# Feed-forward behind a blocked attention: from feature rows to token rows, on one core

## The chip, the core and the metric

The kernel runs on 1 core of one Trainium2 chip. The metric is the device time of one execution in microseconds (us): lower is better. The core has TensorE (PE, matrix products), VectorE (DVE), ScalarE (ACT), GpSimd (POOL), SyncE (SP, which here issues the transfers) and 16 DMA engines. Matrix products land in PSUM, which has 8 banks of 128 partitions by 2 KB; everything else works from SBUF, 128 partitions.

## The reference

A linear attention with decay, in blocks, whose output is the input of a highway feed-forward.

```
q, k, v: [4, 8, 768, 64] f32          lam: [8]
for each block of 64 positions:
    intra = (qb @ kb.T * Dmask) @ vb          Dmask[i, j] = lam ** (i - j) for i >= j, else 0
    inter = (qb * lam ** (pos + 1)) @ kv_state
    out[block] = intra + inter
    kv_state = lam ** 64 * kv_state + (kb * lam ** (63 - pos)).T @ vb
x = out, as [3072 tokens, 512 features]
H = maximum(x @ w_h, 0)
T = 1 / (1 + exp(-(x @ w_t + b_t)))
result = T * H + (1 - T) * x                  f32, [3072, 512]
```

The result can be written as (H - x) * T + x, which is how both kernels do it.

## The kernel before

The 3072 tokens are cut into 12 tiles of 256 (4 batches of 3). Every instruction is issued in an order written out by hand: the string PLAN is a list of tokens, each a step with its tile, its part, after "@" its engine, and after "=" its PSUM banks (0 to 6; a further bank holds the state kv). Each engine runs its own instructions in this order, and so does SP's DMA queue with its loads and stores; an instruction that waits holds up all that stand behind it on its engine.

The steps of a tile: `Lk`, `Lq`, `Lv` load the inputs in two halves of 4 heads, 256 KB each (`load`, line 173; each contiguous run is 2 tokens of one head, 512 bytes). `CK` casts k to bf16; `CQ` and `CV` scale q and v by powers of lambda (`scale`, line 190), on POOL mostly. `TK` and `TQ` turn k and q on PE, eight transposes each (`trans`, line 204); `EK` and `EQ` copy them out of the bank (lines 101 for ACT, 103 for the others). `SS` makes the scores of one half of the heads together with updates of the state (lines 216, 221); `M` masks the scores on DVE (line 255); `KE` copies the state out; `I` and `A` make the inter and intra parts of the output (lines 271, 281); `D` copies it to xT, with features in partitions and tokens in the free dimension, and permutes the tokens while it writes.

Feed-forward: `W` loads the two weights (line 177), four loads of 512 KB in 2 KB rows; `WC` casts them. `F` is `block` (line 300): a 128x128 piece of a weight is the stationary operand and 256 tokens of xT stream past it, 8 matmuls for a bank of two feature groups; 4 blocks a tile, two for each weight. `H` is `relu` (line 305): max(h, 0) - xT, from the bank and SBUF. `G` is the sigmoid (line 314), two instructions a block, with the bias as one number for each partition, back into the bank. `X` is the gate (line 318), which reads that bank. `R` turns xT and the gated th back into token rows on PE, adding them in the bank (line 347; 327 for the last tile, which goes in two halves of 128 tokens). `E` copies the result out, `ST` stores it (lines 356 and 337), from SP.

`Z` are idle matmuls of 512 columns (line 366), which keep PE busy while it waits at the start. The SBUF tiles rotate through the numbers of buffers in BUFS; five each for the loaded q, k and v.

Of the kernel before, what the change touches and what calls it, by code (L numbers as in the profile page):

```python
# [17 lines left out]
Lk.0.0 Lv.0.1 Lv.0.0 Lq.0.0 Lk.0.1 Lq.0.1 Lv.1.1 CK.0.0@POOL Lq.1.0 Z.12=0 TK.0.0=0 Lq.1.1 CV.0.0@DVE Lk.1.0  # L18
CQ.0.0@POOL EK.0.0@DVE Lv.1.0 CV.0.1@DVE CK.0.1@ACT Lk.1.1 Z.11=1 TQ.0.0=1 B=2 EQ.0.0@ACT CQ.0.1@POOL W.0.1 W.0.0
Z.6=0 TQ.0.1=3 TK.0.1=4 EQ.0.1@DVE U.0.0 EK.0.1@ACT W.1.1 S.0.0=56 KE.0.0@DVE S.0.1=01 CQ.1.2@POOL W.1.0 M.0.0.1 Z.1=3  # L20
U.0.1 I.0=34 M.0.1.1 KE.0.1@ACT Lk.2.1 M.0.0.0 A.0.1 M.0.1.0 TQ.1.2=0 Lq.2.1 CV.1.2@DVE CK.1.2@ACT EQ.1.2@ACT Lq.2.0
Z.8=1 TK.1.2=1 A.0.0 EK.1.2@DVE Lk.2.0 D.0.0@DVE Z.3=5 SS.1.1=56 WC.0.0.1@ACT WC.0.0.0@POOL M.1.1.0 KE.1.0@ACT
WC.0.1.0@POOL D.0.1@ACT Lv.2.1 WC.0.1.1@DVE Z.4=0 SS.1.0=01 M.1.1.1 I.1=35 KE.1.1@ACT Lv.2.0 F.0.0.0=4 WC.1.1.0@DVE PT
M.1.0.1 Lk.3.1 F.0.1.0=6 M.1.0.0 WC.1.0.0@POOL WC.1.0.1@ACT Lk.3.0 WC.1.1.1@DVE A.1.1 A.1.0 BC F.0.0.1=1 H.0.1 Lq.3.1
D.1.1@ACT H.0.0 D.1.0@ACT F.0.1.1=0 Lq.3.0 CQ.2.2@POOL F.1.0.0=2 Lv.3.0 G.0.1@ACT CK.2.2@DVE F.1.0.1=6 Lv.3.1
G.0.0@ACT X.0.1@DVE TQ.2.2=5 Lq.4.0 X.0.0@DVE TK.2.2=4 EQ.2.2@ACT CV.2.2@POOL F.1.1.0=3 Lq.4.1 EK.2.2@DVE G.1.0@ACT
H.1.0 SS.2.0=01 Lk.4.1 H.1.1 CK.3.2@POOL SS.2.1=54 Lk.4.0 M.2.0.1 F.1.1.1=2 KE.2.0@ACT M.2.1.0 Lv.4.0 TK.3.2=3 M.2.1.1
CQ.3.2@POOL G.1.1@ACT I.2=15 M.2.0.0 Lv.4.1 A.2.1 X.1.0@DVE A.2.0 Lk.5.0 R.0=40 D.2.0@ACT D.2.1@DVE CV.3.2@POOL
TQ.3.2=6 E.0.0@ACT Lk.5.1 F.2.1.1=1 E.0.1@ACT EQ.3.2@DVE Lq.5.1 EK.3.2@ACT X.1.1@DVE F.2.1.0=5 CQ.4.2@POOL Lq.5.0
R.1=40 H.2.1 SS.3.1=62 Lv.5.0 F.2.0.0=3 CK.4.2@POOL KE.3.0@ACT M.3.1.1 Lv.5.1 E.1.1@ACT M.3.1.0 SS.3.0=52 E.1.0@ACT  # L30
H.2.0 Lq.6.0 TQ.4.2=0 KE.3.1@ACT CV.4.2@POOL M.3.0.1 TK.4.2=6 G.2.1@ACT Lq.6.1 F.2.0.1=4 M.3.0.0 EQ.4.2@ACT EK.4.2@DVE
Lv.6.0 I.3=32 A.3.0 CK.5.2@POOL A.3.1 Lk.6.1 SS.4.1=56 D.3.0@ACT D.3.1@DVE TK.5.2=0 KE.4.0@ACT M.4.1.1 Lk.6.0
F.3.0.0=2 G.2.0@ACT CQ.5.2@POOL EK.5.2@DVE Lv.6.1 SS.4.0=36 H.3.0 F.3.0.1=0 Lq.8.0 M.4.0.0 CV.5.2@POOL M.4.0.1
TQ.5.2=2 Lk.9.0 G.3.0@ACT F.3.1.0=3 X.2.1@DVE Lq.7.0 EQ.5.2@ACT X.2.0@DVE F.3.1.1=6 CQ.6.2@POOL M.4.1.0 Lq.7.1
KE.4.1@ACT I.4=14 H.3.1 G.3.1@ACT R.2=25 Lk.8.1 X.3.0@DVE A.4.0 E.2.1@ACT X.3.1@DVE A.4.1 Lk.7.1 SS.5.0=30 E.2.0@ACT
D.4.0@DVE CK.6.2@POOL SS.5.1=56 D.4.1@ACT Lk.7.0 TQ.6.2=2 M.5.0.0 KE.5.0@ACT CV.6.2@POOL TK.6.2=1 M.5.1.1 Lv.7.0
EQ.6.2@ACT F.4.1.0=4 M.5.0.1 Lv.7.1 EK.6.2@ACT F.4.0.0=3 H.4.1 Lk.8.0 M.5.1.0 I.5=62 SS.6.1=01 H.4.0 Lq.8.1 A.5.0
KE.6.0@ACT M.6.1.0 CQ.7.2@POOL R.3=45 Lv.9.1 A.5.1 M.6.1.1 SS.6.0=30 D.5.0@ACT Lv.8.0 F.4.0.1=1 M.6.0.0 D.5.1@ACT
M.6.0.1 Lk.9.1 TQ.7.2=6 G.4.0@ACT CK.7.2@POOL F.5.0.0=3 Lq.10.1 EQ.7.2@ACT F.4.1.1=2 H.5.0 Lk.10.1 E.3.1@ACT X.4.0@DVE
TK.7.2=0 CV.7.2@POOL G.4.1@ACT I.6=63 ST.0 KE.6.1@DVE F.5.0.1=5 X.4.1@DVE Lv.8.1 F.5.1.0=1 G.5.0@ACT CK.8.2@POOL  # L40
EK.7.2@DVE Lq.9.0 A.6.0 E.3.0@ACT H.5.1 A.6.1 SS.7.1=20 Lq.9.1 D.6.0@ACT D.6.1@DVE TK.8.2=4 M.7.1.1 F.6.1.0=1 Lv.9.0
EK.8.2@ACT X.5.0@DVE CK.9.2@POOL F.6.1.1=6 KE.7.0@DVE Lk.10.0 CQ.8.2@POOL H.6.1 R.4=30 SS.7.0=54 Lk.11.1 E.4.0@ACT
F.5.1.1=1 E.4.1@ACT M.7.0.1 G.6.1@ACT ST.4 M.7.1.0 TK.9.2=3 Lq.10.0 M.7.0.0 TQ.8.2=0 G.5.1@ACT CV.8.2@POOL F.6.0.0=4
EQ.8.2@DVE Lk.11.0 KE.7.1@ACT X.5.1@DVE I.7=25 EK.9.2@ACT Lq.11.0 A.7.0 H.6.0 A.7.1 CQ.9.2@POOL SS.8.0=01 X.6.1@DVE
D.7.1@ACT Lv.10.1 SS.8.1=34 M.8.0.1 D.7.0@ACT F.6.0.1=6 KE.8.0@DVE Lq.11.1 CK.10.2@POOL F.7.0.0=5 M.8.1.0 G.6.0@ACT
M.8.1.1 ST.3 TQ.9.2=1 CV.9.2@POOL H.7.0 F.7.1.0=2 EQ.9.2@ACT Lv.10.0 X.6.0@DVE TK.10.2=3 M.8.0.0 ST.1 I.8=45
EK.10.2@ACT CQ.10.2@POOL H.7.1 SS.9.1=61 A.8.1 KE.9.0@ACT M.9.1.0 A.8.0 R.5=02 M.9.1.1 SS.9.0=36 CK.11.2@POOL
E.5.1@DVE F.7.0.1=1 KE.9.1@ACT M.9.0.1 E.5.0@ACT F.7.1.1=2 D.8.0@DVE D.8.1@ACT ST.5 CQ.11.2@POOL M.9.0.0 G.7.0@ACT
Lv.11.1 TK.11.2=6 Lv.11.0 I.9=04 F.8.1.0=5 EK.11.2@ACT ST.2 X.7.0@DVE TQ.10.2=3 G.7.1@ACT H.8.1 CV.10.2@POOL F.8.0.0=1
EQ.10.2@ACT R.6=65 H.8.0 A.9.1 X.7.1@DVE A.9.0 SS.10.1=31 D.9.0@ACT D.9.1@DVE F.8.1.1=2 E.6.1@ACT M.10.1.1 F.9.1.0=0  # L50
E.6.0@DVE G.8.1@ACT M.10.1.0 ST.6 TQ.11.2=4 CV.11.2@POOL KE.10.0@DVE F.9.1.1=5 EQ.11.2@ACT X.8.1@DVE SS.10.0=16
G.9.1@ACT H.9.1 R.7=32 M.10.0.1 KE.10.1@ACT F.8.0.1=4 X.9.1@DVE E.7.0@ACT M.10.0.0 E.7.1@ACT I.10=06 SS.11.0=53
G.8.0@ACT ST.7 A.10.0 M.11.0.0 A.10.1 SS.11.1=21 D.10.1@ACT X.8.0@DVE F.9.0.0=5 KE.11.0@ACT M.11.1.0 D.10.0@ACT
F.9.0.1=6 M.11.0.1 M.11.1.1 F.10.1.0=4 G.9.0@ACT H.9.0 I.11=20 X.9.0@DVE A.11.0 A.11.1 R.8=31 D.11.0@ACT R.9=56
E.8.0@ACT F.10.0.0=2 E.9.0@DVE E.9.1@ACT E.8.1@ACT D.11.1@DVE ST.9 F.10.1.1=3 H.10.0 ST.8 F.10.0.1=6 H.10.1 G.10.1@ACT
F.12.1.1=5 G.10.0@ACT X.10.1@DVE F.11.1.1=1 F.11.1.0=0 G.12.1@ACT X.10.0@DVE F.11.0.1=2 G.11.1@ACT H.11.1 F.12.1.0=4
R.10=36 G.11.0@ACT H.12.1 X.11.1@DVE F.11.0.0=0 E.10.0@ACT X.12.1@DVE F.12.0.1=4 E.10.1@ACT H.11.0 F.12.0.0=1
G.12.0@ACT X.11.0@DVE ST.10 R.11.1.1=5 H.12.0 R.11.0.2=3 E.11.1.1@DVE X.12.0@DVE E.11.0.2@ACT ST.11.1.1 R.11.1.0=0
ST.11.0.2 E.11.1.0@DVE ST.11.1.0
"""  # L60

BUFS = dict(kf=5, qf=5, vf=5, kb=3, qb=2, vs=3, kT=2, qT=2, m=8, xT4=2, th4=2, xT2=3, xT1=2, th2=2, th1=2, hm2=3, hm1=2, tb2=2, tb1=2, ss=4, o=5, oh=2, oq=1)
# [3 lines left out]
def kernel(  # L66
# [18 lines left out]
    J = 2  # L85
    N = B * NST
# [19 lines left out]
    lam_bc = singles.tile([128, H], F32)  # L106
    A.dma_start(out=lam_bc, in_=lam.partition_broadcast(128))
    bt_r = singles.tile([KC, 128], F32)
    A.dma_start(out=bt_r, in_=moe_b_t.rearrange("(j p) -> j p", p=128))
    id128 = singles.tile([128, 128], BF16)  # L110
    make_identity(nc, id128)
    blank = singles.tile([128, 512], BF16)
    V.memset(blank, 0.0)
    tk_i = singles.tile([128, NST, J], I32)
    P.iota(tk_i, pattern=[[2 * C, NST], [1, J]], base=0, channel_multiplier=J)
    tri = singles.tile([128, J, J, C // J], F32)
    P.memset(tri, 1.0)
    for b in range(2):
        P.affine_select(out=tri[half(b)], in_=tri[half(b)], compare_op=ALU.is_ge, fill=0.0, base=0,
                        pattern=[[-1, J], [1, J], [J, C // J]], channel_multiplier=-J)  # L120
    tri = tri.rearrange("p j i q -> p j (i q)")
    tk_f = singles.tile([128, NST, J], F32)
    V.tensor_copy(tk_f, tk_i)
    id_f = singles.tile([KC, KC], F32)
    V.tensor_copy(id_f, id128[0:KC, 0:KC])
    A.preload_act_table_set("natural_log_exp_and_others")
    ln_bc = singles.tile([128, H], F32)
    A.activation(ln_bc, lam_bc, AF.Ln)
    p_ln = singles.tile([128, NST, H, J], F32)
    V.tensor_tensor(p_ln, in0=ln_bc[:, None, :, None].to_broadcast([128, NST, H, J]),  # L130
                    in1=tk_f[:, :, None, :].to_broadcast([128, NST, H, J]), op=ALU.mult)
    pow_q = singles.tile([128, NST, H, J], F32)
    A.activation(pow_q, p_ln, AF.Exp)
    pow_v = singles.tile([128, NST, H, J], F32)
    A.activation(pow_v, p_ln, AF.Exp, scale=-1.0)
    bt_col = singles.tile([128, KC], F32)
# [4 lines left out]
    kv = ps.tile([128, NP, 128], F32, tag="kv", name="kv", bufs=1)  # L141
    V.memset(kv, 0.0)


    made = {}

    def groups(n, b):
        return ((n,), b) if n < N - 1 else ((n, b), 0)
# [12 lines left out]
    def get(*key):  # L161
        return made[key]
# [7 lines left out]
    def load(x, n, p, eng):  # L170
        b, c = divmod(n, NST)
        hs = heads(p)
        (A if eng else nc.sync).dma_start(out=new((x + "f", n), [128, H, J * D], F32)[:, hs],  # L173
                          in_=SRC[x][b, hs, c * 2 * C:(c + 1) * 2 * C, :].rearrange("h (p j) d -> p h (j d)", j=J))

# [7 lines left out]
    def cast_k(n, p, eng):  # L183
        hs = heads(p)
        copy(eng, new(("kb", n), [128, J, H, D])[:, :, hs].rearrange("p j h d -> p h j d"),
             get("kf", n)[:, hs].rearrange("p h (j d) -> p h j d", j=J))

    def scale(n, p, eng, src, dst, pw):
        z = H if p == 2 else 4
        ENG[eng].tensor_tensor(dst, in0=get(src, n)[:, heads(p)].rearrange("p h (j d) -> p h j d", j=J),  # L190
                               in1=pw[:, n % NST, heads(p), :, None].to_broadcast([128, z, J, D]), op=ALU.mult)

    def cast_q(n, p, eng):
        scale(n, p, eng, "qf", new(("qb", n), [128, J, H, D])[:, :, heads(p)].rearrange("p j h d -> p h j d"), pow_q)

    def cast_v(n, p, eng):
        scale(n, p, eng, "vf", new(("vs", n), [128, H, J, D])[:, heads(p)], pow_v)

# [220 lines left out]
```

## Time and profile before

| | us |
|---|---|
| median of 3 runs | 109.54 |
| lowest and highest run | 109.3 and 109.64 |
| span of the profiled execution | 109.3 |
| line 300 (feed-forward matmuls) in the chain of waits | 28% of the span |
| loads of q in the chain of waits | 11% |
| idle matmuls, busy time and count | 11.8, 43 |
| masks on DVE, busy time and count | 31.1, 48 |
| scalings of q and v on POOL, busy time | 42.6 |

How to read it: a busy time is the time in which an engine had an instruction running; instructions of an engine may overlap a little, so a group's count times its mean can exceed its busy time. The chain of waits is followed back from the last instruction: its shares add to the span. The table in slices of time gives, for 40 equal slices of 2.73 us, each engine's busy tenths (9 is 90% or more), and the DMA engines' mean busy share. HBM reads are 20.98 MB, writes 6.29 MB.

### The profile page before, as it was taken

Reading aid. Unit: us, or ns where it says so; the run is one execution under the profiler, and the core shown is the slowest. Engines: PE = TensorE matmul, PEld = TensorE weight load, DVE = VectorE, ACT = ScalarE, POOL = GpSimd, SP = SyncE. Lnnn points to the kernel's source line nnn. Section 1 sums busy time; section 2 is a strip of 40 time slices with the busy share of each in tenths; the row PEclk is TensorE's granted clock in tenths of the full one; section 3 lists DMA queues with packets and bytes.
Section 4 is the critical chain, followed back from the end, with each engine's and each line's share of the span. In section 5 each row is a group of like instructions: output and inputs, shape, how many; then the busy total and the mean of one; then the engine's idle time right before and its main releaser. Section 6 shows DMA issues by size and latency. Waiting matters only on the chain.

```text
span 109.3 us, 4968 instructions
## 1 busy us (share of the span) xinstructions
PE 99.4 (91%) x2188; PEld 80.6 (74%) x2190; DVE 82.7 (76%) x140; ACT 71.9 (66%) x129; POOL 55.7 (51%) x46
## 2 busy tenths in 40 slices
PE   4986989899999999999999999998999599999950
PEld 1343654688887878889899889896888478899940
DVE  1241595878998696999977989999858958958960
ACT  3304263787866489499579749975696758776940
POOL 6029420427979858959468296499691600000000
PEclk9999999999999999999999999999999999999999
DMA  0899999999999999989999999599999413207264
GB/s 5 233 304 290 291 366 386 312 290 287 290 266 304 287 250 262 302 228 289 296 300 293 305 341 270 181 346 326 321 333 323 170 69 125 73 6 296 94 233 151
DMA packets 42701, 27.59 MB, mean 252 GB/s; under 512 B 1588, under 2 KB 38712, under 8 KB 42680
## 3 DMA queue, kind: packets, MB, share of 16 engines
q1 hardware_dynamic: 42528, 27.27, 85.1%
q8 instruction: 17, 0.28, 1.2%
q14 instruction: 4, 0.03, 0.1%
q10 hardware_dynamic: 152, 0.01, 0.1%
HBM read 20.98 MB, written 6.29 MB: 249 GB/s over the span
## 4 chain that ended last, share of the span: by engine, by line
PE 61%; DMA 11%; DVE 6%; POOL 5%; ACT 5%; issue 4%; SPq 4%; POOLq 0%; DVEq 0%
PE bt L300 15%; PE bh L300 13%; DMA qf<-in_q_dram 11%; PE bs L216 7%; PE bo L281 5%; PE bx L347 5%; PE bspin L366 4%; PE bqtr L204 4%; DVE m L255 3%; SPq L173 3%; PE bktr L204 3%; POOL qb L190 3%; PE bo L271 3%; ACT qT L101 2%; POOL vs L190 2%
## 5 line engine op out<-in xcount | busy, mean ns | idle before, releaser
L300 PEld LDWEIGHTS <-w_b 128*128 128x128 bf16 x416 | 36.3, 98 | 6.4 <-issue 1.8
L255 DVE TENSOR_TENSOR m<-bs,tri 128x512 bf16<-128x512 f32 x48 | 31.1, 682 | 3.8 <-PE bs L216 3.4
L190 POOL TENSOR_TENSOR qb<-qf,pow_q 128x1024 bf16<-128x1024 f32 (+1 forms) x13 | 23.6, 1813 | 11.2 <-DMA qf<-in_q_dram 10.6
L314 ACT ACTIVATE bt<-bt,bt_col 128x256 f32<-128x256 f32 (+1 forms) x52 | 22.0, 432 | 6.9 <-PE bt L300 4.2
L300 PE MATMUL bt<-xT,w_b 128*128 128x256 bf16 (+1 forms) x208 | 24.5, 265 | 1.3 <-ACT qT L101 1.3
L300 PE MATMUL bh<-xT,w_b 128*128 128x256 bf16 (+1 forms) x208 | 25.0, 265 | 0.2 <-issue 0.2
L190 POOL TENSOR_TENSOR vs<-vf,pow_v 128x1024 bf16<-128x1024 f32 x10 | 19.0, 1904 | 5.0 <-DMA vf<-in_v_dram 4.6
L305 DVE SCALAR_TENSOR_TENSOR hm<-bh,xT 128x512 bf16<-128x512 f32 (+1 forms) x26 | 16.5, 643 | 4.0 <-PE bh L300 2.5
L318 DVE TENSOR_TENSOR th<-bt,hm 128x512 bf16<-128x512 f32 (+1 forms) x26 | 16.5, 643 | 2.1 <-ACT bt L314 2.0
L216 PE MATMUL bs<-qT,kT 64*64 64x128 bf16 x384 | 14.2, 218 | 0.6 <-issue 0.3
L101 ACT ACTIVATE xT<-bo 128x512 bf16<-128x512 f32 x16 | 11.5, 749 | 4.6 <-PE bo L281 4.6
L103 POOL CAST kb<-kf 128x1024 bf16<-128x1024 f32 (+1 forms) x10 | 10.0, 995 | 8.1 <-DMA kf<-in_k_dram 6.8
L101 ACT ACTIVATE ss<-kv 128x512 bf16<-128x512 f32 x15 | 8.9, 595 | 7.3 <-PE bs L216 6.1
L366 PE MATMUL bspin<-blank,id 128*128 128x512 bf16 x43 | 11.8, 416 | 1.6 <-POOL id masks.py:199 1.4
L216 PEld LDWEIGHTS <-kT 64*64 64x64 bf16 x384 | 11.0, 106 | 2.9 <-issue 1.4
L101 ACT ACTIVATE o<-bx 128x512 f32<-128x512 f32 x19 | 10.4, 596 | 1.4 <-PE bx L347 1.3
L101 ACT ACTIVATE qT<-bqtr 128x1024 bf16<-128x1024 bf16 (+1 forms) x10 | 9.8, 980 | 1.8 <-PE bqtr L204 1.8
L281 PE MATMUL bo<-m,vs 64*64 64x128 bf16 x384 | 9.4, 219 | 0.7 <-DVE m L255 0.4
L221 PE MATMUL kv<-vs,kb 64*64 64x64 bf16 x320 | 9.2, 196 | 0.2 <-POOL vs L190 0.2
L366 PEld LDWEIGHTS <-id 128*128 128x128 bf16 x45 | 4.3, 105 | 6.4 <-issue 1.7
L204 PE MATMUL bqtr<-id,qb 128*128 128x128 bf16 x96 | 7.5, 220 | 0.9 <-POOL qb L190 0.9
L281 PEld LDWEIGHTS <-vs 64*64 64x64 bf16 x384 | 6.6, 106 | 2.4 <-issue 1.5
(50 smaller groups left out, 109.1 us busy)
## 6 DMA issues: line engine op xcount, KB each, us to landing
kf<-in_k_dram SPq DMA_DIRECT2D x24, 256.0 KB, 5.5
vf<-in_v_dram SPq DMA_DIRECT2D x24, 256.0 KB, 5.4
qf<-in_q_dram SPq DMA_DIRECT2D x24, 256.0 KB, 5.5
out_dram<-o SPq DMA_DIRECT2D x11, 512.0 KB, 4.7
w_f<-in_moe_w_h_dram SPq DMA_DIRECT2D x2, 512.0 KB, 6.6
w_f<-in_moe_w_t_dram SPq DMA_DIRECT2D x2, 512.0 KB, 8.5
out_dram<-oh SPq DMA_DIRECT2D x2, 128.0 KB, 2.0
out_dram<-oq SPq DMA_DIRECT2D x1, 256.0 KB
```

The costliest lines, as they stand in the source:

```text
L101: A.activation(dst, src, AF.Copy)
L103: ENG[eng].tensor_copy(dst, src)
L190: ENG[eng].tensor_tensor(dst, in0=get(src, n)[:, heads(p)].rearrange("p h (j d) -> p h j d", j=J), in1=pw[:, n % NST, heads(p), :, None].t ...
L204: T.transpose(t[:, i, j, :], get(x + "b", n)[:, j, h:h + 2, :], id128)
L216: T.matmul(get("s", n, e, hp // 2)[half(b), hp % 2, j, :], lhsT=get("kT", n)[half(e), hp, j, half(b)], rhs=get("qT", n)[half(e), hp, :, ha ...
L255: V.tensor_tensor(new(("m", n, e, u), [128, 2, J, C]), in0=get("s", n, e, u), in1=tri[:, None].to_broadcast([128, 2, J, C]), op=ALU.mult)
L281: T.matmul(get("o", n, b)[half(e), hp, :], lhsT=get("vs", n)[half(b), 2 * hp + e, j, :], rhs=get("m", n, e, u)[half(b), hp % 2, j, :], sta ...
L300: T.matmul(t[:, r, :], lhsT=w_b[w][:, kc, (2 * u + r) * 128:(2 * u + r + 1) * 128], rhs=get("xT", *g)[:, kc, :], start=(kc == 0), stop=(kc ...
L305: V.scalar_tensor_tensor(new(("hm", g, u), [128, 2, z * C], tag=f"hm{z}"), in0=get("h", g, u), scalar=0.0, in1=get("xT", *g)[:, 2 * u:2 * ...
L314: A.activation(dst[:, r, :], src[:, r, :], AF.Sigmoid, bias=bt_col[:, 2 * u + r:2 * u + r + 1])
L318: ENG[eng].tensor_tensor(new(("th", g), [128, NP, z * C], tag=f"th{z}")[:, 2 * u:2 * u + 2, :], in0=get("tt", g, u), in1=get("hm", g, u), ...
L366: T.matmul(t, lhsT=id128, rhs=blank, start=True, stop=True)
```

## The change

The feed-forward is computed in token rows. For 128 tokens at a time, xT is the stationary operand and 512 columns of a weight stream past it (`block`: 4 matmuls for a bank of 128 tokens by 512 features; parts of 256 columns for the end of the last tile). The result needs no turning back. Instead x itself is turned once (`TX`, `rows`: eight transposes a tile, and `XC`, `evac_x`, a copy to SBUF in bf16).

The bias now runs along the free dimension, so it is written into the bank before the matmuls add to it (`BP`, `begin`): a copy of a 128x512 tile b_bc on ACT (20 times) or DVE (5 times). b_bc is made at the start from three bf16 parts of the bias in a weight tile, by one matmul with ones (`B`, `BB`, `BC`).

`H` writes max(h, 0) - x to y in f32; `G` is one sigmoid instruction of 512 columns without a bias operand, to g in SBUF in f32; `X` multiplies y by g and `Y` adds x, both with all operands in SBUF, on DVE (8 and 12 times) or POOL (17 and 13 times). `ST` stores a tile, five times in two transfers of 119 and 9 rows.

q is loaded in runs of 8 tokens of one head (2 KB), with 32 groups of tokens and 4 heads over the partitions; powers of lambda are laid out to match (pow_q8), the turned q is put in order when it is copied out (`EQ`, strided read, written in order), and `D` copies without a permutation. Lambda is loaded as 8 numbers and spread over the partitions by two small matmuls. Four more idle matmuls stand at the start; the Z tokens have 23 in place of 45.

The order is new: all loads of tiles 0 to 3 stand ahead of the weights, and the feed-forward begins after the inter part of tile 3. Scalings are spread differently (8 of 12 whole scalings of q on POOL before 11, 6 of v before 10).

```diff
-BUFS = dict(..., m=8, xT4=2, th4=2, xT2=3, xT1=2, th2=2, th1=2, hm2=3, hm1=2, tb2=2, tb1=2, ss=4, o=5, oh=2, oq=1)
+BUFS = dict(..., m=8, ss=4, xT=3, xs=3, y=4, g=3, ob=5)
...
+        if x == "q":
+            nc.sync.dma_start(out=new(("qf", n), [128, 2, Q * D], F32)[:, p],
+                              in_=q[b].rearrange("(h e) (c p j) d -> c e p h (j d)", e=2, p=C // NP, j=Q)[c, p])
+            return
...
     def evac_q(n, p, eng):
-        hs = heads(p)
-        copy(eng, new(("qT", n), [128, NP, J, C])[:, hs.start // 2:hs.stop // 2], get("qtr", n, p))
+        hs = slice(0, NP) if p == 2 else slice(2 * p, 2 * p + 2)
+        copy(eng, new(("qT", n), [128, NP, 2 * C])[:, hs].rearrange("e h (p j) -> e h p j", j=Q),
+             get("qtr", n, 2).rearrange("e j (p h) -> e h p j", h=NP)[:, hs])
...
+    def rows(n, p, bk):
+        bs = range(2) if p == 2 else (p,)
+        t = bank(("x", n, p), bk[0], [C, len(bs), KC, 128], BF16)
+        for i, b in enumerate(bs):
+            for j in range(KC):
+                T.transpose(t[:, i, j, :], get("xT", n)[:, j, b * C:(b + 1) * C], id128)
...
-    def block(i, u, w, bk):
-        g, z = group(i)
-        t = bank(("ht"[w], g, u), bk[0], [128, 2, z * C])
-        for r in range(2):
-            for kc in range(KC):
-                T.matmul(t[:, r, :], lhsT=w_b[w][:, kc, (2 * u + r) * 128:(2 * u + r + 1) * 128],
-                         rhs=get("xT", *g)[:, kc, :], start=(kc == 0), stop=(kc == KC - 1))
+    def block(n, b, w, p, bk):
+        z = cols(p)
+        t = get("t", n, b, p) if w else bank(("h", n, b, p), bk[0], [C, z.stop - z.start])
+        for j in range(KC):
+            T.matmul(t, lhsT=get("xT", n)[:, j, b * C:(b + 1) * C], rhs=w_b[w][:, j, z], start=(j == 0 and not w), stop=(j == KC - 1),
+                     skip_group_check=True)
+
+    def begin(n, b, p, eng, bk):
+        z = cols(p)
+        t = bank(("t", n, b, p), bk[0], [C, z.stop - z.start])
+        if eng:
+            copy(eng, t, b_bc[:, z])
+        else:
+            T.matmul(t, lhsT=row1, rhs=b_w[:, z], start=True, stop=False, skip_group_check=True)
...
+    def sigm(n, b, p):
+        z = cols(p)
+        A.activation(new(("g", n, b), [C, DM], F32)[:, z], get("t", n, b, p), AF.Sigmoid)
+
+    def gate(n, b, p, eng):
+        z = cols(p)
+        y = get("y", n, b)[:, z]
+        ENG[eng].tensor_tensor(y, in0=y, in1=get("g", n, b)[:, z], op=ALU.mult)
+
+    def total(n, b, p, eng):
+        z = cols(p)
+        o = new(("o_sb", n), [C, 2, DM], F32, tag="ob")[:, b, z]
+        ENG[eng].tensor_tensor(o, in0=get("y", n, b)[:, z], in1=get("xr", n, b)[:, z], op=ALU.add)
+
+    def store(n, parts):
+        i = 2 * n * C
+        for p in parts:
+            nc.sync.dma_start(out=out[i:i + 2 * C].rearrange("(b p) f -> p b f", p=C)[p], in_=get("o_sb", n)[p])
```

The new order, at the places that the prediction speaks of:

```diff
+... Lk.3.0 Lv.3.1 Lv.3.0 PT@ACT CV.0.0@POOL CV.0.1@DVE U.0.0 W.0.0 W.0.1 W.1.1 W.1.0 Lk.4.1 ...
+... I.3=41 D.2.0@ACT F.0.1.0.2=5 Lv.7.0 WC.1.0.1@POOL KE.3.1@DVE Lk.7.0 F.1.0.0.2=2 H.1.0.2@DVE H.0.1.2@DVE
+TX.2.2=6 XC.2.2@ACT F.1.1.0.2=3 H.1.1.2@DVE CK.4.2@DVE BP.0.1.2@ACT=2 BP.1.0.2@ACT=5 BP.1.1.2@ACT=3 F.0.0.0.2=0 ...
+... F.11.1.1.0 G.11.1.0@ACT H.11.1.0@DVE X.11.1.0@DVE
+Y.11.1.0@DVE ST.11.1.0
```

## The prediction

> **What bounds the kernel now.** First the busy times and the 40 slices, then the chain of waits, then a table of 5 us stretches, then groups by shape, last the timeline of two places.
>
> ```profile
> span 109.3 us, 4968 instructions
> PE 99.4 (91%) x2188; PEld 80.6 (74%) x2190; DVE 82.7 (76%) x140; ACT 71.9 (66%) x129; POOL 55.7 (51%) x46
> ...
> POOL 6029420427979858959468296499691600000000
> ...
> DMA  0899999999999999989999999599999413207264
> ...
> PE 61%; DMA 11%; DVE 6%; POOL 5%; ACT 5%; issue 4%; SPq 4%; POOLq 0%; DVEq 0%
> ```
>
> TensorE (PE) is busy 91% and is 61% of the chain; DMA is full until slice 31 (85 us), then idle. The stretches tell when each of the two sets the pace:
>
> ```profile
> 5.00:10.00 5.00, 3.57 (x22) 1.45 (x19) 2.09 (x4) 0.92 (x3) 2.41 (x3) 1.00 1.19 303
> 10.00:15.00 5.00, 4.65 (x103) 2.96 (x102) 2.83 (x5) 1.79 (x3) 2.73 (x2) 1.00 1.18 305
> 15.00:20.00 5.00, 4.61 (x77) 2.73 (x77) 3.55 (x6) 2.66 (x4) 1.04 (x2) 1.00 1.06 379
> 20.00:25.00 5.00, 4.92 (x97) 3.78 (x97) 4.33 (x10) 4.24 (x6) 1.43 (x3) 1.00 1.17 294
> ...
> 45.00:50.00 5.00, 5.00 (x138) 4.59 (x140) 5.00 (x10) 4.02 (x8) 3.86 (x3) 1.00 0.95 267
> ...
> 85.00:90.00 5.00, 3.74 (x92) 3.05 (x90) 3.71 (x7) 3.20 (x6) 1.78 (x1) 1.00 0.33 120
> ```
>
> Columns: PE, weight load, DVE (VectorE), ACT (ScalarE), POOL, then clock, DMA share, GB/s. Until some 21 us PE is filled with idle matmuls (L366) and waits for loads; from there to 105 it is close to gapless, with 1.84 us idle between 70 and 90, where the chain runs through a late load of q into POOL. So: loads set the start, PE the rest. The clock is 1.00 throughout and explains nothing.
>
> **PE's sum, before.** Spacing in unbroken runs of the chain: eight 256-column matmuls take 0.87 us, eight transposes 0.45, scores with states 0.60, inter 0.45 (0.22 in a batch's first tile), half an intra 0.285, a turning back 0.57. Over the order of tokens: feed-forward 41.9, transposes 10.8, scores and states 14.4, inter 4.5, intra 6.8, turning back 6.8: 85.2 us. At 27.1 us the order has 10.8 behind it (the fifth feed-forward block); the other 74.4 take until PE's last matmul at 105.8: 78.7 us, 94.5%. Without the 1.84 us of late loads: 96.7%.
>
> **Part by part.**
>
> *Feed-forward stream.* 32 matmuls of 256 columns a tile become 16 of 512. Idle matmuls of 512 columns, warm: seven take 1.67 us, three 0.81, so 0.215 each against 2 x 0.109. 192 x 0.215 = 41.3: -0.6 us. Half the weight loads go; they are hidden already (98 ns under 109) and give nothing.
>
> *Turning.*
> ```profile
> L347 PE MATMUL bx<-id,xT 64*128 64x64 bf16 x176 | 6.6, 191 | 0.0
> L347 PE MATMUL bx<-id,th 64*128 64x64 bf16 x176 | 6.5, 190 | 0.0
> ```
> 0.57 a tile becomes eight transposes, 0.45: 12 x 0.12 = -1.4 us. One spreading matmul for the bias: +0.2. PE's new sum: 83.4.
>
> *Elementwise work, 256 tokens.* Before: DVE 4 x 0.683, ACT 4 x 0.449 and two outputs of 0.596. After: on ACT two sigmoids without bias pointer (between the 0.595 of a 512-wide copy from the bank and 2 x 0.449; I take 0.61, nearest the copy), bias copies into the bank (ACT 0.595 to 0.629, the 512-wide rows; 0.60; 20 there, 5 on DVE at 0.69) and one copy of x (1.03); on DVE two relus (0.69); then two gates and two sums, all operands in SBUF: 20 on DVE (0.69, as its 512-wide scaling of v), 30 on POOL (1.04, as its 512-wide scaling of q; the other such row has 1.58, see below). `take` without its permuted write goes from 0.749 to 0.595. Sums over all tokens: DVE 89.2 to 94.3, ACT 77.0 to 81.4, POOL 53.8 to 70.4. Back-to-back instructions overlap (DVE: 82.7 busy for 89.4 added up over its rows, 0.925). The bias copies sit in ACT's and DVE's order ahead of other work; the h block of 0.87 us covers each. Uncovered, 25 x 0.6 = 15 us.
>
> *q in rows of 8 tokens.* The 512-byte runs move at 288 to 305 GB/s; the stretch with the weights, 2 KB runs, has 379. So q goes at 295 (nothing gained) to 379. I take 379, the row with the same run length. The new copy of qT reads strided: 1.03, or up to 0.31 more (the permuted `take` pays 0.15 on 512 elements); 0 to 3.4 us on ACT, which has room (63.9 x 0.925 = 59 of the 73 us after 28.3); on the path once at most, for tile 3.
>
> By the Trainium skill's page "DMA: Bandwidth & Descriptors" (Specifications), 512 B is already enough for the line rate; then longer rows would bring nothing, and the second rival below would hold. The two rows above speak against it.
>
> *New order.* The weights stand behind all loads of tiles 0 to 3 (24 on SP's queue instead of 12), and the feed-forward begins after inter(3). Bytes ahead: k and v 4.19 MB at 295 = 14.2 us, q 2.10 and w_h 1.05 at 379 = 8.3; first bytes at 3.0 us. That is 25.5. In the trace w_h's last byte is the 4.19th MB, moved at 16.7 by the slices, and its first cast starts at 18.9: +2.2. A cast of 0.63: first feed-forward matmul at **28.3 us**. The order has 12.7 us of PE work ahead of it, which fits; w_t comes 2.8 later, covered by four h blocks (3.5). All that is new at the start (lambda by matmul, bias rows, iotas, fewer idle matmuls) hides behind these weights. Uncovered, it costs what it delays tile 3.
>
> *Later queues.* By rates, loads are ahead of their casts from tile 5 on: tile 7's last by 49 us, its cast at 53. The stores that stand ahead of loads (tile 1's before q of tile 9) have data at about 47 us, SP reaches them near 55: no wait. POOL's sums stand in its order behind scalings that wait for loads; a late load would now hold gates too, and through three buffers of g the sigmoid and its bank. With loads ahead: nothing.
>
> *Tail.* From the last matmul: sigmoid 0.45, gate 0.42, sum 0.42, store as before (output copy done 106.28, end 109.3) 3.0, hops 0.1: 4.4.
>
> **Sum.** 83.4 - 12.7 = 70.7 us of PE work from 28.3. The loads that cost the 1.84 us are ahead now, so 96.7%: 73.1. 28.3 + 73.1 + 4.4 = 105.8. The median before stands 0.2 over its profiled span: **106.0 us**. Own range: gapless PE 103.6; before's 94.5% 107.7, and with the weights half as late as in the second rival 108.9.
>
> **Rivals.**
>
> *VectorE becomes the bound, through the port.* Two places show that some DVE instructions and POOL's exclude each other:
> ```profile
> 25.14 1.63 DVE L103 CAST kb<-kf 128x1024 bf16<-128x1024 f32 x1
> ...
> 24.32 1.91 POOL L190 TENSOR_TENSOR qb<-qf,pow_q 128x1024 bf16<-128x1024 f32 x1 [2.14 <-DMA qf<-in_q_dram]
> ...
> 8.05 1.58 POOL L190 TENSOR_TENSOR qb<-qf,pow_q 128x512 bf16<-128x512 f32 x1 [2.11 <-DMA qf<-in_q_dram]
> 9.78 1.04 POOL L190 TENSOR_TENSOR qb<-qf,pow_q 128x512 bf16<-128x512 f32 x1 [0.16 <-DMA qf<-in_q_dram]
> ```
> The cast ends 0.5 after POOL's instruction ends at 26.23 (alone about 0.69, from the 512-wide 0.418). POOL's scaling that starts 10 ns after a DVE scaling of v takes 0.54 more. Before, masks, relus and gates read a bank and one SBUF tensor, so this happened rarely. After the first feed-forward block 27 DVE instructions (20 gates and sums, 5 scalings, 2 casts) read only SBUF, while POOL is busy 57.7 of 74 us. Met at random: 27 x 0.78 x a mean rest of 0.67 (from lengths 1.9 and 1.04) = 14.1 us of waiting. DVE's own rest is 71.7 x 0.925 = 66.3. At 97% busy: 28.3 + 80.4/0.97 + 3.0 = 114.2, **114.4**. It decides from 9.4 us of waiting on, two thirds of chance meetings; below 6.0 PE hides it. For: DVE has 90% load already, and masks queue behind a waiting gate, intra behind masks. Against: the order can place these instructions where POOL idles.
>
> The Trainium skill's "SBUF — State Buffer" (Who interferes with whom) says that a DVE instruction with two SBUF inputs and a GpSimd one reading SBUF block each other entirely. The two places agree.
>
> *The weights come late.* q at 295 too: 7.34/0.295 = 24.9 + 3.0 + 2.2 + 0.6 = 30.7, 2.4 later: 108.2, **108.4** with the 0.2. The change doesn't do with q what it says. For: DMA share 1.18 at the 512-byte runs says the engines are full, not that rows are slow. Against: 379.
>
> *PE without gaps:* 28.3 + 70.7 + 4.4 + 0.2 = **103.6**. For: 45 to 50 us and others are at 5.00. Against: DVE at 90%.
>
> **Chances.** Forecast 53%, port 32% (109.5 to 114.4 by how many meet), late weights 8%, gapless 7%. A measurement here tells 0.3% from no change, 109.2 to 109.9. Faster: 0.51 + 0.06 + 0.07 = 0.64; same: 0.02 + 0.02 + 0.01 = 0.05; slower 0.31. The range 103.0 to 113.0 leaves out the worst third of the port case and a little below 103.6; the forecast's own is 103.6 to 108.9.
>
> **What would show it.** Right: first w_h matmul near 28.3; PE 5.00 in most stretches from 30 on; 512-column matmuls 0.215 apart; the slices with q above 305 GB/s; last matmul near 101. Wrong: DVE gates, sums or scalings well over 0.69 or POOL's over 1.04 where they overlap, with PE idle on masks (port); first w_h after 30 (weights). Not foreseen by any case: PE waiting on a bank for a bias copy, or POOL waiting on loads with gates behind it.

## The result and the profile after

The changed kernel takes 119.5 us (median of 4 runs, 118.34 to 124.53), the kernel before 109.42 (4 runs, 108.67 to 109.64). The ratio is 1.0831, 95% interval 1.077 to 1.0891: slower by 9 us (118.34 and 118.48 against 109.42). The forecast was 106.0, range 103.0 to 113.0: wrong in sign and outside its range. The runs at 120.53 and 124.53 had a lower granted clock (0.97 and 0.935, against 0.987 and 0.996) and are not in the ratio; the profile is of the run at 118.34.

The page of the changed kernel, its busy times and two of its rows of slices:

```profile
span 116.6 us, 3994 instructions
...
PE 95.9 (82%) x1670; PEld 60.6 (52%) x1688; DVE 102.3 (88%) x148; ACT 75.6 (65%) x120; POOL 88.1 (76%) x72
...
POOL 7236766703753999999999899999999996619660
...
DMA  2999999999999999999986799950000244682472
```

PE fell from 91% to 82%, DVE rose from 76% to 88%, and POOL, 51% before, is full from slice 14 to 33 (with one 8). DMA is mostly full until slice 26 (near 75 us) and then nearly idle for a while. The stretches of 5 us (columns: PE, weight load, DVE, ACT, POOL, clock, DMA share, GB/s):

```profile
40.00:45.00 5.00, 3.87 (x111) 2.65 (x112) 5.00 (x6) 4.41 (x9) 4.92 (x3) 1.00 1.08 324
45.00:50.00 5.00, 4.95 (x94) 3.25 (x93) 4.59 (x7) 2.85 (x5) 5.00 (x4) 1.00 1.10 298
50.00:55.00 5.00, 3.53 (x60) 2.75 (x54) 4.41 (x5) 4.03 (x7) 5.00 (x5) 1.00 1.02 334
...
85.00:90.00 5.00, 4.61 (x105) 3.31 (x95) 4.94 (x7) 4.14 (x7) 5.00 (x4) 1.00 0.01 3
```

The kernel before has in two of these stretches:

```profile
40.00:45.00 5.00, 5.00 (x139) 4.28 (x137) 4.14 (x8) 4.08 (x8) 3.67 (x3) 1.00 0.95 272
...
50.00:55.00 5.00, 5.00 (x162) 4.47 (x155) 4.92 (x9) 3.69 (x6) 3.49 (x3) 1.00 1.03 287
```

PE is not gapless where it was before: 3.87 and 3.53 stand beside a DVE and a POOL at 4.4 to 5.00. From 85 to 90 nothing is loaded, and PE still has gaps. The clock is 1.00 in all of them. Why DVE and POOL are full is in the groups by shape (L421 is the gate, L426 the sum, L244 the scaling of v, L238 that of q, L341 the mask, L114 copies and casts, L256 the turning of k and q):

```profile
L421 POOL TENSOR_TENSOR y<-y,g 128x512 f32<-128x512 f32 x16 | 25.6, 1602 | 5.5 <-DVE y L411 3.6 <-ACT g L416 1.8
...
L426 POOL TENSOR_TENSOR ob<-y,xs 128x512 f32<-128x512 f32 x12 | 16.8, 1412 | 2.8 <-DVE y L421 2.5
...
L426 DVE TENSOR_TENSOR ob<-y,xs 128x512 f32<-128x512 f32 x11 | 11.8, 1082 | 0.6 <-POOL y L421 0.5
...
L244 DVE TENSOR_TENSOR vs<-vf,pow_v 128x1024 bf16<-128x1024 f32 x5 | 8.6, 1712 | 0.0
...
L421 DVE TENSOR_TENSOR y<-y,g 128x512 f32<-128x512 f32 x7 | 7.4, 1059 | 0.3
```

The forecast had 0.69 for a gate or sum on DVE (here 1.06 and 1.08) and 1.04 on POOL (here 1.60 and 1.41). Masks and relus, which read a bank, kept their 0.68. One meeting in the timeline (start, length):

```profile
76.14 1.89 POOL L244 TENSOR_TENSOR vs<-vf,pow_v 128x1024 bf16<-128x1024 f32 x1
...
76.33 2.25 DVE L421 TENSOR_TENSOR y<-y,g 128x512 f32<-128x512 f32 x1
...
78.50 0.68 DVE L341 TENSOR_TENSOR m<-bs,tri 128x512 bf16<-128x512 f32 x1
```

The gate on DVE begins 0.19 after POOL's scaling, takes 2.25 instead of 0.69, and ends 0.55 after it. The mask behind it comes 1.6 late. And the chain of waits, in order of time, shows what a full POOL does to PE (followed back from the end it reaches only to 70.1 us):

```profile
73.29 1.90 POOL qb L238
75.19 0.98 POOL kb L114
76.17 1.86 POOL vs L244
78.03 1.68 POOL y L421
79.71 0.99 POOL kb L114
...
80.75 0.62 PE bktr L256 x8
```

POOL runs without a pause for 7.4 us, and a gate of 1.68 stands ahead of the cast of k that PE waits to turn. None of these waits for a load.

### The profile page after: what moved, and what is told of

It reads as the page before. It is cut to its first block, busy times and chain, and to the rows that moved or that the text cites. A ratio compares the mean times of both kernels' runs of the same rounds, so it can differ in the third digit from the quotient of the medians.

```text
span 116.6 us, 3994 instructions
## 1 busy us (share of the span) xinstructions
PE 95.9 (82%) x1670; PEld 60.6 (52%) x1688; DVE 102.3 (88%) x148; ACT 75.6 (65%) x120; POOL 88.1 (76%) x72
## 5 line engine op out<-in xcount | busy, mean ns | idle before, releaser
L341 DVE TENSOR_TENSOR m<-bs,tri 128x512 bf16<-128x512 f32 x48 | 30.7, 681 | 3.5 <-PE kv L289 2.1
L421 POOL TENSOR_TENSOR y<-y,g 128x512 f32<-128x512 f32 (+1 forms) x17 | 26.6, 1569 | 6.5 <-DVE y L411 4.7
L398 PEld LDWEIGHTS <-xT 128*128 128x128 bf16 x200 | 18.3, 98 | 20.4 <-issue 3.6
L398 PE MATMUL bt<-w_b,xT 128*128 128x512 bf16 (+1 forms) x92 | 23.6, 370 | 2.0 <-ACT bt L112 1.3
L398 PE MATMUL bh<-w_b,xT 128*128 128x512 bf16 (+1 forms) x93 | 23.3, 370 | 1.0 <-issue 0.6
L238 POOL TENSOR_TENSOR qb<-qf,pow_q 128x1024 bf16<-128x1024 f32 (+1 forms) x9 | 17.6, 1963 | 6.9 <-DMA qf<-in_q_dram 3.2
L416 ACT ACTIVATE g<-bt 128x512 f32<-128x512 f32 (+1 forms) x25 | 14.4, 582 | 9.0 <-PE bt L398 5.9
L426 POOL TENSOR_TENSOR ob<-y,xs 128x512 f32<-128x512 f32 (+1 forms) x13 | 17.6, 1359 | 2.8 <-DVE y L421 2.5
L411 DVE SCALAR_TENSOR_TENSOR y<-bh,xs 128x512 f32<-128x512 f32 (+1 forms) x25 | 16.2, 661 | 1.5 <-PE bh L398 1.0
L112 ACT ACTIVATE bt<-b_bc 128x512 f32<-128x512 f32 (+1 forms) x20 | 11.7, 595 | 4.7 <-DVE y L411 4.6
L244 POOL TENSOR_TENSOR vs<-vf,pow_v 128x1024 bf16<-128x1024 f32 (+1 forms) x7 | 12.5, 1788 | 2.3 <-ACT kT L112 1.8
L426 DVE TENSOR_TENSOR ob<-y,xs 128x512 f32<-128x512 f32 (+1 forms) x12 | 12.6, 1057 | 0.6 <-POOL y L421 0.5
L114 POOL CAST kb<-kf 128x1024 bf16<-128x1024 f32 x8 | 9.1, 1142 | 1.2 <-PE bo L363 0.6
L244 DVE TENSOR_TENSOR vs<-vf,pow_v 128x1024 bf16<-128x1024 f32 (+1 forms) x6 | 9.8, 1636 | 0.0
L256 PE MATMUL bqtr<-id,qb 128*128 128x128 bf16 x96 | 7.3, 219 | 2.7 <-DVE qb L238 1.2
```

The lines of the kernel that those rows point to most:

```text
L112: A.activation(dst, src, AF.Copy)
L114: ENG[eng].tensor_copy(dst, src)
L238: ENG[eng].tensor_tensor(new(("qb", n), [128, Q, 2, D])[:, :, es].rearrange("p j e d -> p e j d"), in0=get("qf", n)[:, es].rearrange("p e ...
L244: ENG[eng].tensor_tensor(new(("vs", n), [128, H, J, D])[:, heads(p)], in0=get("vf", n)[:, heads(p)].rearrange("p h (j d) -> p h j d", j=J) ...
L341: V.tensor_tensor(new(("m", n, e, u), [128, 2, J, C]), in0=get("s", n, e, u), in1=tri[:, None].to_broadcast([128, 2, J, C]), op=ALU.mult)
L398: T.matmul(t, lhsT=get("xT", n)[:, j, b * C:(b + 1) * C], rhs=w_b[w][:, j, z], start=(j == 0 and not w), stop=(j == KC - 1), skip_group_ch ...
```

## The experiments

Theory: POOL and DVE instructions that read SBUF hold each other up when they run at the same time (a meeting, below), and that makes both engines the bound. Rivals: POOL is simply too full; the order of a split chain (relu, gate, sum on two engines) is at fault; bank or bias copies hold PE up; the q part or the start.

**e4_port: the disputed cost by itself.** Products of 128x512, first on each engine by itself, then ten on both at once, with other operands from group to group (a and the bf16 tile h are in SBUF, pa is in PSUM, which DVE reads as well):

```
for _ in range(10):
    tt(P, pf, a[0], a[1])
    tt(V, vf, a[0], a[1])
...
for _ in range(10):
    tt(P, pf, a[0], a[1])
    tt(V, vf, pa, a[1])
...
for _ in range(20):
    P.memset(pf, 1.0)
for _ in range(10):
    tt(V, vf, a[0], a[1])
```

> The disputed prices by themselves; nothing of the reference is computed. 128x512 products in stages: POOL alone with each kind of operands, VectorE alone with each kind, then both at once: VectorE with two SBUF operands; VectorE with one PSUM and one SBUF operand; VectorE with two SBUF operands beside POOL memsets; at last VectorE casts and bf16 products beside POOL. Port theory: alone POOL 1.04 (bf16 out) to 1.27 us (f32 out), VectorE 0.68; both at once with two SBUF operands they take turns, a pair costs the sum, 1.7 to 1.9 us, so each instruction shows its own time plus a wait; with a PSUM operand, or beside memsets, each keeps its time alone. Rival (POOL's gates and sums are simply slower than the scalings, and VectorE waits for semaphores, not for a port): durations in the stages with both are those of the stages alone.

In the timeline of this kernel:

```profile
2.02 5.28 POOL L32 TENSOR_TENSOR pf<-a,a 128x512 f32<-128x512 f32 x4 [1.58 <-DVE a L21]
...
41.01 15.94 POOL L32 TENSOR_TENSOR pf<-a,a 128x512 f32<-128x512 f32 x10
...
44.19 14.76 DVE L32 TENSOR_TENSOR vf<-a,a 128x512 f32<-128x512 f32 x10
...
61.11 7.22 DVE L32 TENSOR_TENSOR vf<-pa,a 128x512 f32<-128x512 f32 x10
...
76.59 7.23 DVE L32 TENSOR_TENSOR vf<-a,a 128x512 f32<-128x512 f32 x10
76.61 11.58 POOL L59 MEMSET pf<- 128x512 f32 x20 [0.79 <-DVE vf L32]
...
96.23 10.20 DVE L32 TENSOR_TENSOR vg<-h,h 128x512 bf16<-128x512 bf16 x10
```

A single product of two full f32 tensors takes POOL 1.26, and 1.32 in a row, not 1.04: the rows that gave 1.04 have one operand repeated along the row. With both engines reading SBUF twice, ten take DVE 14.8 and POOL 15.9. Two of each were undisturbed, at POOL's start and at DVE's end; the eight that met took DVE 13.30 and POOL 13.26, which is 1.66 for each pair, against 0.69 and 1.26 alone. With a bank as one of DVE's inputs, or with POOL only writing, DVE's ten take 7.2: nothing is lost. A product of bf16 loses too: the last four ran after POOL had ended, and the six before them took 8.36, 1.39 each against 0.43 alone.

The Trainium skill's "SBUF — State Buffer" (Who interferes with whom) has the same three cases: a DVE instruction with two SBUF inputs and a GpSimd one that reads SBUF conflict, one with a single SBUF input doesn't (outside the two-port modes that it lists), and a GpSimd instruction that only writes doesn't. The rows agree, but for the degree: the Trainium skill has the loser block fully, and of a pair that would take 0.69 + 1.26 = 1.95 one after the other 1.66 is left, so something overlaps.

**e2_memset: POOL as full, but reading nothing.** POOL's 17 gates and 13 sums are left out, and memsets of like length stand in their places.

```diff
+        if eng == "POOL":
+            P.memset(y, 0.5)
+            P.memset(get("g", n, b)[:, z], 0.5)
+            P.memset(y[:, 0:192 if p == 2 else 48], 0.5)
+            return
```

> The changed kernel, with POOL's 17 gates and 13 sums replaced by memsets of about the same length (so those products and sums are left out), which write but read nothing from SBUF; same place in the order, same waits on h, the sigmoid and buffers. Port theory: without the reads VectorE's gates and sums go back to 0.68 and the kernel falls from 118.3 by 6 us or more, to 107 to 112. Rival, load alone (POOL with 30 more instructions is simply full): POOL stays as full, the time stays within 2 us of 118.3. Rival, order (weights late, attention first): no change either.

111.98 us (111.64 to 112.26), ratio 1.0257 [1.021, 1.0304]. Groups on DVE (L436 is the sum here, L426 the gate):

```profile
L436 DVE TENSOR_TENSOR ob<-y,xs 128x512 f32<-128x512 f32 x11 | 8.0, 737 | 0.0
L426 DVE TENSOR_TENSOR y<-y,g 128x512 f32<-128x512 f32 x7 | 4.8, 682 | 0.7 <-ACT g L416 0.6
```

Gates and sums are back at 0.68 and 0.74. POOL is still busy 78.7 us of the 109.9, in unbroken stretches, and its scalings still read: DVE's scalings of v take 1.84 beside them. So 5.7 points of the 8.3% go with the reads of these 30 instructions, and a full POOL by itself is not the loss.

**e7_inplace: a control.** y is computed in the output tile, with the output in 8 buffers. The next kernels need this, so that a left-out step leaves no tile unwritten.

> Control for the next two, complete computation: the changed kernel with y kept in the output tile (gates and sums in place, 8 output tiles, no tile y). Same instructions on the same engines. All theories: 117 to 119.5, as the changed kernel. If it is faster by over 1.5 us, waits for y's four or the output's five buffers were part of the loss.

118.31 us (118.09 to 118.6), ratio 1.083 [1.0786, 1.0874]: as the changed kernel, with eight buffers where y had four and the output five. So the buffers of y and of the output are not the cause; the three of g were left as they are.

**e8_pool_free, e9_dve_free, e11_both_free: gates and sums left out** of the control on POOL (30), on DVE (20), and on both (50). Two memsets of 8 columns stand for each. The diff is that of the gates for POOL; the others are alike.

```diff
+        if eng == "POOL":
+            P.memset(y[:, 0:8], 0.5)
+            P.memset(get("g", n, b)[:, z][:, 0:8], 0.5)
+            return
```

> As the control, but POOL's 17 gates and 13 sums are left out (memsets of 8 columns in their place). With their reads alone gone, the memset run had 112.0. If POOL's length was the rest of the loss: 106 to 109. If the rest is VectorE's own load: 110.5 to 112.5, with VectorE 5.00 of 5 in most stretches and POOL half idle.

> As the control, but VectorE's 8 gates and 12 sums are left out (memsets of 8 columns). It takes away 13.7 us of VectorE's own and the waits of both sides at these 20 places; 5 scalings and 2 casts there still meet POOL. Port theory: 107 to 111, POOL's gates back at 1.27. If POOL's own length of 37 us for gates and sums binds: 113 to 117.

> The control with the gates and sums left out on both engines (50 instructions become memsets of 8 columns, two for each, in the same places of the order). Theory, that these 50 instructions with their meetings at the port are all that holds PE up after its start: PE starts the feed-forward near 30 as before, its 70.7 us then take 73.1 (96.7%), the tail without gate and sum 3.6, and some 2 us lie around the span: 108 to 109, first of PE's stretches from 35 on at 4.8 and more. Rival, that the order itself (scalings and casts behind one another, sigmoid, bias copies, masks) holds PE at some 94% whatever gates and sums cost: 111 to 112, as with the memsets of full length on POOL (111.98).

Ratios to before: 1.031 [1.0243, 1.0377] without POOL's, 1.0353 [1.0296, 1.0411] without DVE's, 1.001 [0.995, 1.007] without either. Without POOL's 30 the kernel is no faster than with memsets of their length in e2_memset (1.0257): beyond their reads, POOL's time for them cost nothing that these runs can tell, as long as DVE's are in. Either side alone gives back 5 points. Were meetings between the two groups the whole loss, either side alone would give back all of it. The other 3 points go only when both are out, and what they are was not separated: the load itself, or meetings with the scalings, which go on in all three kernels. The theory's 107 to 111 for e9_dve_free was missed (median 113.19), which lies where POOL's own length was expected to bind. Without either group the loss is gone, and no gain appears. Stretches of the last kernel, columns as above:

```profile
45.00:50.00 5.00, 5.00 (x114) 3.62 (x114) 4.98 (x6) 4.39 (x9) 3.60 (x11) 1.00 1.08 302
50.00:55.00 5.00, 4.78 (x102) 3.35 (x101) 4.89 (x8) 4.44 (x6) 1.21 (x4) 1.00 1.11 331
...
85.00:90.00 5.00, 4.95 (x96) 2.76 (x96) 4.26 (x7) 3.04 (x6) 0.42 (x6) 1.00 0.48 115
```

PE's idle time has closed: from its first w_h matmul at 30.99 to its last at 103.67 are 72.7 us for the forecast's 70.7 of work, 97.2%.

**e3_bank_gate: gates that can't meet POOL.** 14 sigmoids are written back into the bank, and DVE's gate reads it there; all 25 sums but two go to POOL, and six of the gates stand earlier in the order.

```diff
-        A.activation(new(("g", n, b), [C, DM], F32)[:, z], get("t", n, b, p), AF.Sigmoid)
+        dst = get("t", n, b, p) if (n, b, p) in BANK else new(("g", n, b), [C, DM], F32)[:, z]
+        made["gg", n, b, p] = dst
+        A.activation(dst, get("t", n, b, p), AF.Sigmoid)
```

> The changed kernel with 14 of 25 sigmoids written back into their bank, and those gates on VectorE, which reads the bank and one SBUF operand; 22... of 25 sums on POOL, the other gates where they were. Complete computation. VectorE has about as many gates and sums as before this edit, POOL fewer gates and more sums. Port theory: fewer meetings, 110 to 115. Load alone: POOL's load is nearly the same (11 gates and 23 sums), so 117 to 119.

120.65 us (119.47 to 122.43): not faster, since even its shortest run is above the changed kernel's 118.34. Both expectations, 110 to 115 and 117 to 119, were missed. The gates from the bank take 0.69, as the theory says, but two waits have grown (total, times, longest):

```profile
POOL ob L430 <- DVE y L425: 7.0, 5, 2.4
ACT bt L114 <- DVE y L425: 5.5, 4, 2.9
```

In the changed kernel POOL's sums waited 2.5 us for DVE's gates, and ACT's bias copies 4.6 for DVE's relus. Now the sums wait 7.0, with scalings behind them; and a bank is held until DVE has gated, so the bias copy for the next block waits for the gate. Meetings of gates were removed, and the time that this freed seems to have gone into these waits; the two effects were not taken apart.

**e5_bf16 and e10_split: bf16, and one engine for each step.** y and g in bf16, all gates on DVE, 23 sums on POOL (e5_bf16); in e10_split also five scalings from DVE to POOL and two casts of k from DVE to ACT.

```diff
-        V.scalar_tensor_tensor(new(("y", n, b), [C, DM], F32)[:, z], in0=get("h", n, b, p), scalar=0.0,
+        V.scalar_tensor_tensor(new(("y", n, b), [C, DM])[:, z], in0=get("h", n, b, p), scalar=0.0,
...
-H.9.1.2@DVE X.9.1.2@POOL BP.11.1.1@DVE=0 Y.10.1.2@DVE
+H.9.1.2@DVE X.9.1.2@DVE BP.11.1.1@DVE=0 Y.10.1.2@POOL
```

> Complete computation, same order: y and g in bf16; all 25 gates on VectorE (measured alone 0.43 us for bf16 products), 23 sums on POOL, 2 on VectorE; the 5 scalings that VectorE had after tile 3 on POOL, its two casts of k on ACT. VectorE's SBUF-only time falls from some 24 us to 12, POOL's from 58 us to about 52. Port theory: the loss shrinks by half or more, 108 to 113. If order or PE were the cause: 116 to 119.

> The changed kernel with y and g in bf16, all 25 gates on DVE and 23 of 25 sums on POOL, and the scalings and casts where the changed kernel has them (the kernel that split further had moved five scalings to POOL and two casts to ACT as well: 124.4). If moving the scalings made that one slow, this one is 115 to 118.5. If it is the split of gate and sum over two engines (POOL waits in order for DVE's gates, and its scalings stand behind), it is 121 or more, and POOL's sums wait for DVE's gates for over 10 us in all.

e10_split: 124.37 us (122.37 to 125.77), ratio 1.124 [1.1162, 1.1317]; e5_bf16: 119.51 (119.33 to 120.68), ratio 1.0948 [1.0882, 1.1014]. The theory's 108 to 113 for e10_split was far off. Waits there:

```profile
POOL ob L426 <- DVE y L421: 19.2, 10, 5.0
...
DVE y L411 <- PE bh L398: 10.0, 11, 5.2
```

POOL's sums wait 19.2 us for gates, the scalings that PE needs stand behind them, and DVE then waits for PE. With the scalings left on DVE (e5_bf16) the same wait is still 17.3 in all, but costs only 1.2 points over the changed kernel. e5_bf16 met the wait that was expected of a costly split (over 10 us), but not its time (121 or more). So e10_split's loss seems to be two things: the split itself, and moving what PE needs onto the engine that waits. A third is not separated from them: the granted clock fell in both for 10 us (0.58 and 0.74 from 55 to 65 us in e10_split, 0.74 and 0.58 from 50 to 60 in e5_bf16), where the changed kernel has 1.00. A gate in bf16 takes 0.70 in e5_bf16, against 0.43 alone and 1.06 for the changed kernel's in f32, and the kernel is still not faster.

**e12_bias_pe: the bias by one matmul of 512 columns** in place of the 25 copies, on the control.

```diff
-BP.0.1.2@ACT=2 BP.1.0.2@ACT=5 BP.1.1.2@ACT=3
+BP.0.1.2=2 BP.1.0.2=5 BP.1.1.2=3
```

> The control with the bias put into the bank by one matmul of 512 columns on PE instead of a copy on ACT (20) or DVE (5): PE's sum grows by 25 x 0.215 = 5.4 us, ACT's falls by 20 x 0.60 = 12, DVE's by 5 x 0.69 = 3.5. If the copies stand in the way (an h block can't follow until a bank is filled, and ACT waits for relus to free it), PE gains more than the 5.4 it pays in its idle 9.8 us: 115 to 117.5. If the copies are covered, as the prediction had it, and the port with POOL's prices is the loss, the 5.4 us go partly into PE's idle time: 118 to 121.

121.03 us (120.43 to 121.65), ratio 1.1065 [1.0997, 1.1133]: 2.7 slower than the control, for 5.4 more on PE. Sigmoids on ACT now wait 17.4 us for PE's banks. Of the 5.4, 2.7 do not show: either PE did them in its idle time, or leaving out the copies gave them back. So the copies are at most 2.7 of the 9 us of loss. In the changed kernel PE waited for one three times, 1.7 us in all, a wait that the prediction listed as foreseen by no case.

**e1_q_rows: the q part alone**, on the kernel before: 2 KB rows, the strided copy of the turned q, lambda by matmul, q of the first tile turned in one step, and other idle matmuls at the start.

```diff
+        if x == "q":
+            nc.sync.dma_start(out=new(("qf", n), [128, 2, Q * D], F32)[:, p],
+                              in_=q[b].rearrange("(h e) (c p j) d -> c e p h (j d)", e=2, p=C // NP, j=Q)[c, p])
+            return
```

> The kernel before with one part of the change alone: q loaded in runs of 8 tokens, its powers and lambda made as in the changed kernel, qT put in order by the copy out, xT copied without permutation; feed-forward and order as before. If 2 KB rows move faster (the changed kernel shows 330 GB/s at the start where before had 303), the late loads between 70 and 90 us shrink: 107.5 to 109.0. If rows of 512 B were no limit: 109.0 to 109.9. If the strided copy out of qT costs: above 110.

110.61 us (109.8 to 112.04), ratio 1.0103 [1.0049, 1.0157]. Its stretches:

```profile
5.00:10.00 5.00, 4.94 (x22) 2.08 (x20) 2.48 (x3) 0.65 (x2) 1.87 (x2) 1.00 1.04 339
10.00:15.00 5.00, 4.37 (x88) 2.87 (x87) 2.58 (x5) 1.77 (x4) 2.12 (x2) 1.00 1.12 342
```

339 and 342 GB/s against 303 and 305 before: these loads are faster, and the kernel is 1% slower: above 110, as it was expected if the strided copy out costs. DVE's two whole copies of that kind take 1.22 each, its copies of a turned k, without strides, 0.69. Which of the part's pieces costs the 1% was not separated.

## Why the prediction failed, step by step

The miss is 118.34 - 106.0 = 12.3 us for the profiled run. Start, PE's stretch and tail, read from the timelines (first w_h matmul, last matmul, span):

| | first w_h | from there to last matmul | tail | around span | time |
|---|---|---|---|---|---|
| forecast | 28.3 | 73.1 | 4.4 | 0.2 | 106.0 |
| changed kernel | 29.9 | 80.5 | 6.2 | 1.7 | 118.3 |
| POOL reads nothing (e2_memset) | 30.4 | 75.0 | 4.5 | 1.7 | 111.6 |
| no gates, no sums (e11_both_free) | 31.0 | 72.7 | 3.6 | 1.7 | 109.0 |

**Where it failed: the prices of the elementwise step, "30 on POOL (1.04, as its 512-wide scaling of q ...)" and "20 on DVE (0.69 ...)".** 7.4 us of the miss are in PE's stretch and 1.8 in the tail. Both prices were those of an instruction that meets nobody, and POOL's came from a row with a repeated operand. POOL's product of two full f32 operands takes 1.26 alone (e4_port), and with the meetings gates and sums took 1.41 to 1.60 there and 1.06 to 1.08 on DVE. In four rows DVE lost 7 x 0.37 + 11 x 0.39 on gates and sums, and with 1.22 for an undisturbed scaling 5 x 0.49 + 3 x 0.42 on those of v and q: 10.6 us. With POOL reading nothing, 5.5 of the 7.4 and 1.7 of the 1.8 go.

**The rival that held was the port, at 32%.** These 10.6 us are past the 9.4 from which it was to decide. It was put behind the forecast with "the order can place these instructions where POOL idles"; POOL, full from slice 14 to 33, had no such places. Its 114.4 was still 4 too low, and came that near in part by luck: it took 14.1 us of waiting on DVE, and with the measured 10.6 its own sum gives 110.8. It shared the forecast's start and the 0.2, which are 3.1 us too low together. The rest it missed because it counted DVE's waits alone, while POOL is held up as well and is the engine whose scalings PE needs; that this makes the rest is argued from the chain, not measured. Of its two places in the trace before, only the scaling has two SBUF inputs. The other is a cast, which has one, and e4_port shows that casts meet POOL too (1.39 each for four in a row, against 0.42).

**"With loads ahead: nothing" for POOL's order.** No load is late there, and yet the chain shows a gate of 1.68 before a cast that PE waits for. In an order this full, one instruction holds another up without any load being late. The experiments that moved gates to DVE show the same coupling from the other side.

**The start, 28.3.** The first cast of w_h ran from 27.43 to 28.19 on POOL, as forecast, so the weights were on time. But PE in its own order came to inter(3) only at 29.71, and another of the first casts ran on ACT until 30.09, behind copies. "The order has 12.7 us of PE work ahead of it, which fits" counted work and not the chain through masks and copies: 1.6 us. Before had 74.4 us of PE work left at 27.1, so 70.7 at some 30.8: the new kernel begins 0.9 us ahead of it, not the 2.5 of the forecast.

**"The median before stands 0.2 over its profiled span."** Runs that list both have 1.7 to 2.1 us around the span (118.34 and 116.6 here; 109.06 and 107.1 for a run of before). The profile of before, span 109.3, was by this of an execution some 2 us longer than the timed ones: 1.5 us of the forecast gain never existed.

**What held.** 512-column matmuls are 0.215 apart (four in 0.86 in the chain). The rate of 96.7% was right for a PE that elementwise work doesn't hold up: 97.2% without gates and sums. The strided copy on ACT costs nothing extra (1.02), and the bias copies are covered but for 1.7 us. The loads run faster than 305 GB/s: 316 to 332 in the stretches from 5 to 25 us. These hold k and v as well; the forecast's own rates, two thirds at 295 and one third at 379, would make 319 there, and the first cast of w_h began at 27.43 where 27.7 was forecast. Even so e11_both_free, without the 50 instructions, only equals before (ratio 1.001): in this order, a cure of these meetings alone would not have made the change a gain. Where the 1.8 us that PE saves go in that kernel stays open, since the profile of before shows a longer execution than the timed ones. No version tried here beats the kernel before; whether another placement of the 50 instructions would was not tried beyond these.

## What to carry to other kernels

Before moving elementwise work from operands in PSUM to operands in SBUF, count on each engine the instructions that read SBUF twice, and price them as met: 1.66 us for a pair of 512-column products here, not 0.69 beside 1.04. An instruction's price comes from a row with the same operands (full or repeated) and from a moment when the neighbour is as busy as it will be. A step split over two engines that work in order ties both to each other; what the bound engine waits for must not stand behind it.

## What the runs showed of the hardware beyond that

- POOL's product by its operands (128x512): 1.04 when one is repeated along the row, 1.26 for two of full f32, 1.15 when one or both are bf16 (four in 4.84 and 4.83, against 5.28). An output in bf16 saves nothing (5.28 as well).
- A DVE cast from f32 to bf16 has one SBUF input and still lost beside POOL's products: the four that met them took 5.57, 1.39 each, against 0.42 for the first, which met none.
- DVE copies a turned q of 1024 bf16 from the bank with strides in 1.22 (e1_q_rows), a turned k without in 0.69; ACT takes 1.02 for both.
